# State-space layer with two routed tokens on one core: another order of the same steps on all engines

## The chip, the core and the metric

The kernel runs on one core of a Trainium2 chip. Its engines each take instructions from a queue of their own, in order: TensorE (PE in the profile), VectorE (DVE), ScalarE (ACT), GpSimd (POOL) and SyncE (SP), which here issues nearly all transfers. What counts is the device time of one execution in microseconds, as the median of the runs. The core runs alone, and the granted clock of TensorE stands at full speed throughout the profile.

## What is computed

The input x has 2048 tokens of 1024 features, the output the same. The reference, cut to what matters (bfloat16 inputs, recurrence over time in its exact form):

```python
xn = layernorm(x)
Lam_bar = exp(dt * Lam); B_bar = ((Lam_bar - 1) / Lam)[:, None] * B     # complex, 1024 states
for t in range(2048):
    h = Lam_bar * h + (B_bar @ xn[t])
    a[t] = 2 * real(C @ h) + xn[t] * Dskip
r = xn @ w_r;  idx = the two tokens with the largest r
b = xn;  b[idx] += sigmoid(r[idx]) * ((silu(xn[idx] @ w_gate) * (xn[idx] @ w_up)) @ w_down)
y = x + a + b
```

## The kernel before, in words

**Stages.** The tokens go through in 8 frames of 256 and 16 chunks of 128. Of frame f, `Bu.f.j` (TensorE, L667, 16 matmuls, eight groups j) multiplies the normalised, transposed tokens by B; `u.f.j` (ScalarE, L673) copies the result from PSUM; `TI.f` (VectorE, L722 and L724) turns it by a table of phases, so that the recurrence becomes a real one. Of chunk c, `SC.c.0.0` and `SC.c.0.1` (VectorE, L750; L743 for chunk 15) are the scans of the real and the imaginary part; `gb.c` (ScalarE, L756) copies each to bfloat16; `cw`, `cy` and `cin` (GpSimd, L766, L774, L781 and L782) carry the state to the next chunk, whose scan needs it; `TO.c` (VectorE, L792 and L794, in pieces of half the groups or less for chunks 0, 1 and 15 at L799 to L801) turns the states back; `Y.c.q` (TensorE, L879, 8 matmuls) multiplies them by C, into one of three PSUM banks that `seed.c.h` (ScalarE, L855) has filled with the residual. `xs.c` (ScalarE, L864) and `xm.c` (VectorE, L869) form the skip term in one of two output buffers, `ADD.c.h` (VectorE, L890) adds half a chunk of the product to it, and `out.c.h` (SP, L894) stores the half. The buffers of `xs.c` are those of chunk c-2, so `xs.c` needs the stores of c-2 landed. The seed that takes a bank needs the addition that emptied it.

**Layer norm.** Chunks 0 to 5 have their statistics on VectorE (`bs`, `bn`, L309 and L312) and are normalised there (`apply`, L338 and L345); of the others ScalarE does both (`sum`, `sq`, `apply`, L318, L324 and L349). `rstd` (L277, L278), `nmean`, `nmr` and `nmr1` are small steps on ScalarE or GpSimd. The first four chunks are transposed by TensorE (`Tpe`, L382 and L387) and copied by ScalarE (`xnT`, L394), the later ones by a transposing transfer on SP (`T.c`, L400). B is transposed by transfers as well (`B.j`, L234). The tables of phases and decay come from small vectors (`pcol`, `wr`, `dt`, `frq`, `sin`, `first`, `cos`, `inv`, `rc`, ...); `rc.0` (VectorE, L547) needs `inv.0` (ScalarE, L543 and L544).

**The two tokens.** `r.f` (TensorE, L408) scores all tokens with the column that `wr` (VectorE, L486) made; `cand` and `idx` (VectorE) find the best two; `gather` (GpSimd, L991) fetches their rows, `xz` (GpSimd, L1017) clears a tile; `bns` (VectorE, L283 and L285), `rstds` (ScalarE, L277 and L278) and `norm` (VectorE, L1012) normalise them, `sT` (SP, L1023) transposes them. The expert weights come in 42 loads `w.n` (SP, L1055 and L1059) and are used in eight visits `mm.i` (TensorE, L1071 and L1102), with `exp`, `gu` and `gT` (ScalarE and VectorE) between. `rows` (ScalarE, L1114) scales the result, `row_.q` (SP, L1117) moves its pieces into one tile. For chunk 15 a product with a selecting matrix adds it in PSUM (`hotY`, L884); for all others `fix` (GpSimd, L1121) adds the two rows to the output by an accumulating transfer, which needs every store of chunks 0 to 14 landed and all pieces moved. The stores of chunk 15 follow it.

**What sets the order.** Every step above is a task with a name. A constant `ORDER` (L25 to L65) lists all tasks by hand; `run` asserts that each stands behind what it needs, and `emit` (L98) issues the instructions of each task in that order. Since the schedule is manual (L125), each engine's queue is the list cut to that engine's tasks, and an engine waits at a task whose input is not ready, with all later ones queued behind it. Semaphores follow the data, so a changed order changes no result.

```python
    def emit(self):
        for n in self.order:
            self.tasks[n]["fn"]()
```

Of the kernel before, what the change touches and what calls it, by code (L numbers as in the profile page):

```python
# [17 lines left out]
T = 128  # L18
# [4 lines left out]
EPS = 1e-5  # L23
NREP = 4
ORDER = """  # L25
x.0 x.1 xa pre start.0 warm.0 warm.1 Bn.1 bs.0 bn.0 rstd.0 nmean.0 nmr1.0 bs.1 applyA apply.0 bn.1 warm.2 warm.3 warm.4 warm.5 warm.6 warm.7 warm.8
warm.9 warm.10 warm.11 warm.12 warm.13 warm.14 warm.15 x.2 TpeA x.3 Tpe.0 xnT0 pP.0 pcol.0 wr xnT.0 Bn.0 tB.0 bs.2 tB.1 rstd.1 apply.1 B.0.0 B.0.1
Tpe.1 Bh.0.0.0 Bh.0.0.1 nmean.1 xnT.1 bs.3 bn.2 rstd.2 nmr1.1 bn.3 nmean.3 B.1.0 apply.2 Bh.0.1.0 B.1.1 Bu.0.0 dt frq Tpe.2 rstd.3 apply.3 Bh.0.1.1
Tpe.3 turns x.4 whole angle abs den B.4.0 Bu.0.1 u.0.0 rad xnT.2 B.2.0 Bh.1.0.0 xnT.3 B.2.1 nmean.2 nmr.2 nmr.0 trig sin B.3.0 first u.0.1 Bh.1.0.1
Bu.1.0 Bu.1.1 Bu.1.2 cos bs.4 bn.4 nmr.1 x.5 bs.5 bn.5 nmr1.3 sq1.0 sq1.1 nmr.3 B.3.1 kappa B.4.1 nmean.4 nmean.5 B.5.0 B.5.1 x.6 B.6.0 u.1.0 B.6.1  # L30
B.7.0 Bu.1.3 u.1.1 log inv.0 rc.0 R0.0 tan.0 u.1.2 inv.1 rc.1 tan.1 B.7.1 cs ts.0.1 u.1.3 rstd.5 rstd.4 apply.4 T.4 xr.0 R0.1 R.1 R.0 Bu.0.2 Bu.0.3
Bu.0.4 nmr1.2 u.0.2 u.0.3 ntan.0 ntan.1 TI.0.0 x.7 E2c.1 xr.2 u.0.4 Bu.0.5 Bu.0.6 sum.6 Bu.0.7 nmean.6 nmr.5 nmr1.4 ends cin.0.0 apply.5 x.9 x.8 u.0.5
T.5 u.0.6 Bu.1.4 xnT.4 SC.0.0.0 nmr.4 sq.6 nmr1.5 SC.0.0.1 Bu.1.5 u.0.7 xs.0 TI.0.4 xnT.5 rstd.6 nmr.6 apply.6 T.6 u.1.4 u.1.5 C.0.0 cw.0.0 cy.0.0
xnT.6 Drow seed.0.0 seed.0.1 ts.0.0 E2c.0 ts.1.0 Bu.1.6 Bu.1.7 Bu.2.0 u.1.6 u.1.7 Bu.2.1 gb.0.0.0 x.12 gb.0.0.1 Bu.2.2 E2n.0 u.2.0 u.2.1 Bu.2.3 Bu.2.4
xr.1 sum.7 u.2.2 Bu.2.5 cin.0.4 SC.0.4.0 gb.0.4.0 SC.0.4.1 C.0.1 cin.1.0 SC.1.0.0 gb.0.4.1 ts.1.1 E2s.1 E2s.0 SC.1.0.1 E2n.1 TO.0.0 TO.0.4 cw.0.4
cy.0.4 u.2.3 Bu.2.6 nmean.7 sq.7 u.2.4 Bu.2.7 rstd.7 nmr.7 apply.7 T.7 gb.1.0.0 cin.1.4 cw.1.0 cy.1.0 xs.1 gb.1.0.1 C.1.0 u.2.5 u.2.6 SC.1.4.0 xm.0
SC.1.4.1 TO.1.0 gb.1.4.0 gb.1.4.1 E2t.1 TO.1.4 u.2.7 sum.9 TI.1.0 C.1.1 sum.8 E2t.0 Y.0.0 Y.0.1 cw.1.4 cy.1.4 cin.2.0 xnT.7 Bu.3.0 seed.1.0 nmean.9
sq.9 nmean.8 rstd.9 Bu.3.1 nmr.9 apply.9 Bu.3.2 u.3.0 u.3.1 cin.2.4 SC.2.0.0 gb.2.0.0 SC.2.0.1 ADD.0.0 sq.8 xm.1 Y.0.2 Y.1.0 Y.1.1 x.10 cw.2.0
gb.2.0.1 Y.0.3 seed.1.1 T.9 sum.12 nmean.12 u.3.2 ADD.1.0 ADD.0.1 out.0.0 TO.2.0 Bu.3.3 Bu.3.4 u.3.3 rstd.8 nmr.8 seed.2.0 Y.1.2 out.0.1 xs.2 Bu.3.5
Bu.3.6 apply.8 w.0 w.1 seed.2.1 T.8 x.15 u.3.4 sq.12 rstd.12 x.11 nmr.12 out.1.0 Y.2.0 Y.2.1 xr.3 cy.2.0 cin.3.0 SC.3.0.0 SC.3.0.1 cw.3.0 cy.3.0 u.3.5  # L40
gb.3.0.0 gb.3.0.1 Y.1.3 cin.4.0 u.3.6 nmr1.6 TI.2.0 ADD.1.1 xm.2 ADD.2.0 apply.12 x.14 sum.10 nmean.10 sq.10 xr.4 SC.4.0.0 cw.4.0 T.12 out.2.0 xnT.9
Bu.3.7 SC.4.0.1 TO.3.0 u.3.7 Y.2.2 rstd.10 nmr.10 gb.4.0.0 xnT.8 Y.2.3 gb.4.0.1 ADD.2.1 TO.4.0 Bu.4.0 Bu.4.1 cy.4.0 cin.5.0 SC.5.0.0 cw.5.0 u.4.0
out.1.1 Bu.4.2 apply.10 T.10 seed.3.0 u.4.1 Bu.4.3 u.4.2 Y.3.0 Y.3.1 sum.11 xs.3 Bu.4.4 Bu.4.5 nmean.11 out.2.1 seed.3.1 seed.4.0 xr.5 SC.5.0.1 sum.15
cy.5.0 cin.6.0 sq.11 nmr1.10 xm.3 gb.5.0.0 rstd.11 ADD.3.0 xs.4 TI.3.0 Y.3.2 Y.3.3 xm.4 seed.4.1 u.4.3 u.4.4 gb.5.0.1 ADD.3.1 x.13 nmean.15 SC.6.0.0
nmr.11 SC.6.0.1 sq.15 rstd.15 Y.4.0 nmr.15 apply.11 apply.15 TO.5.0 gb.6.0.0 Y.4.1 Bu.4.6 u.4.5 Y.4.2 seed.5.0 gb.6.0.1 ADD.4.0 u.4.6 cw.6.0 TO.6.0
Y.4.3 cy.6.0 nmr1.12 cin.7.0 xr.6 SC.7.0.0 cw.7.0 Bu.4.7 ADD.4.1 SC.7.0.1 cy.7.0 cin.8.0 T.11 xnT.11 sum.14 nmean.14 sq.14 xnT.10 Bu.5.0 seed.5.1
u.5.0 Y.5.0 Y.5.1 Y.5.2 Y.5.3 out.3.0 u.4.7 out.3.1 xs.5 xm.5 ADD.5.0 ADD.5.1 T.15 rstd.14 nmr.14 apply.14 TI.4.0 seed.6.0 nmr1.15 gb.7.0.0 xr.7 T.14
Bu.5.1 gb.7.0.1 sum.13 nmean.13 sq.13 rstd.13 nmr.13 out.4.0 Y.6.0 apply.13 Y.6.1 SC.8.0.0 xnT.14 seed.6.1 Bu.5.2 Bu.5.3 u.5.1 SC.8.0.1 Y.6.2 Bu.5.4
out.4.1 out.5.1 u.5.2 TO.7.0 nmr1.11 T.13 xnT.13 xnT.12 cw.8.0 out.5.0 xnT.15 nmr1.9 r.0 cy.8.0 u.5.3 u.5.4 cin.9.0 cand gb.8.0.1 idx Bu.5.5 Y.6.3
nmr1.14 xs.6 xr.8 gb.8.0.0 nmr1.8 xm.6 ADD.6.0 nmr1.7 xs.7 SC.9.0.0 Bu.5.6 Bu.5.7 SC.9.0.1 ADD.6.1 gather w.2 nmr1.13 xz w.3 u.5.5 u.5.6 w.4 u.5.7  # L50
TI.5.0 w.5 seed.7.0 seed.7.1 xr.9 w.6 bns Bu.6.0 Bu.6.1 u.6.0 seed.8.0 Bu.6.2 gb.9.0.1 u.6.1 w.7 xm.7 rstds Y.7.0 Y.7.1 cw.9.0 cy.9.0 out.6.1 out.6.0
ADD.7.0 cin.10.0 Y.7.2 Y.7.3 u.6.2 norm sT ADD.7.1 out.7.1 gb.9.0.0 Bu.6.3 out.7.0 xT ymb0 xs.8 TO.8.0 Bu.6.4 seed.8.1 sig SC.10.0.0 xr.10 xm.8 Bu.6.5
seed.9.0 SC.10.0.1 u.6.3 gb.10.0.0 u.6.4 mm.0 Y.8.0 Y.8.1 ADD.8.0 xs.9 TO.9.0 u.6.5 Y.8.2 Bu.6.6 cw.10.0 cy.10.0 cin.11.0 w.8 w.9 w.10 w.11 out.8.0
seed.9.1 gb.10.0.1 Y.8.3 sig1 xm.9 mm.1 ADD.8.1 SC.11.0.0 SC.11.0.1 u.6.6 exp.0 TO.10.0 cw.11.0 gu.0 gT.0 Bu.6.7 Bu.7.0 Bu.7.1 u.7.0 u.6.7 gb.11.0.0
gb.11.0.1 Y.9.0 hot w.12 w.13 Y.9.1 Y.9.2 out.8.1 w.14 ADD.9.0 w.15 w.16 xs.10 u.7.1 seed.10.0 seed.10.1 cy.11.0 w.17 mm.2 w.18 w.19 exp.1 xr.11 w.20
Bu.7.2 Bu.7.3 w.21 TI.6.0 Y.10.0 u.7.2 Y.9.3 Y.10.1 cin.12.0 SC.12.0.0 Y.10.2 SC.12.0.1 ADD.9.1 seed.11.0 Y.10.3 xm.10 ADD.10.0 gu.1 w.22 w.23 w.24
w.25 TO.11.0 gb.12.0.1 gb.12.0.0 cw.12.0 mm.3 seed.11.1 cy.12.0 ADD.10.1 cin.13.0 SC.13.0.0 SC.13.0.1 out.9.1 out.10.0 gT.1 exp.2 gu.2 gT.2 xr.12
Bu.7.4 Bu.7.5 u.7.3 out.9.0 xs.11 w.26 Y.11.0 Y.11.1 w.27 gb.13.0.1 out.10.1 mm.4 u.7.4 w.28 xm.11 ADD.11.0 cw.13.0 cy.13.0 cin.14.0 Bu.7.6 Bu.7.7
u.7.5 TO.12.0 gb.13.0.0 TO.13.0 Y.11.2 Y.11.3 ADD.11.1 seed.12.0 seed.12.1 xr.13 exp.3 xs.12 u.7.6 Y.12.0 u.7.7 Y.12.1 xm.12 w.29 seed.13.0 w.30 w.31
TI.7.0 ADD.12.0 seed.13.1 w.32 SC.14.0.0 SC.14.0.1 cw.14.0 gb.14.0.0 gb.14.0.1 w.33 w.34 w.35 gu.3 mm.5 Y.12.2 Y.12.3 out.11.0 ADD.12.1 Y.13.0 Y.13.1  # L60
TO.14.0 xr.14 out.11.1 xs.13 seed.14.0 w.36 w.37 gT.3 Y.13.2 Y.13.3 xm.13 ADD.13.0 ADD.13.1 w.38 w.39 w.40 w.41 mm.6 Y.14.0 mm.7 Y.14.1 cy.14.0 xr.15
out.12.1 seed.14.1 cin.15.0 out.12.0 SC.15.6.0 rows xs.14 seed.15.0 out.13.0 out.13.1 SC.15.0.0 SC.15.0.1 TO.15.0 xm.14 ADD.14.0 row_.1 Y.14.2 Y.14.3
ADD.14.1 row_.2 SC.15.4.0 row_.3 ymb xs.15 SC.15.4.1 TO.15.4 Y.15.0 out.14.0 out.14.1 SC.15.6.1 TO.15.6 seed.15.1 hotY.15.0 xm.15 seed.15.2 Y.15.1 fix
Y.15.2 Y.15.3 Y.15.4 Y.15.5 Y.15.6 hotY.15.2 Y.15.7 ADD.15.0 hotY.15.1 ADD.15.1 out.15.0 out.15.1 Y.15.8 ADD.15.2 out.15.2
"""  # L65


# [1116 lines left out]
```

## Time and profile before

| | us |
|---|---|
| median of 3 runs | 252.13 |
| lowest and highest run | 251.70, 252.75 |
| the profiled execution | 251.76 |
| its span in the profile | 250.0 |
| TensorE busy | 243.9 |
| VectorE busy | 238.9 |
| ScalarE busy | 175.8 |
| GpSimd busy | 92.5 |

The span runs from the first to the last instruction on the core; 1.76 us of the execution lie around it. Busy time is the union of an engine's instructions, which overlap a little at their ends; a start and a duration in a row are in microseconds from the start of the span. A row of several instructions of a line (x32) gives first start and total length. A wait in brackets is the idle time of the engine ahead of that row, with what ended it.

### The profile page before, as it was taken

What the parts mean: (1) busy time and instruction counts of PE and PEld (TensorE: products, weight loads), DVE (VectorE), ACT (ScalarE), POOL (GpSimd) and SP (SyncE); (2) the same over time, 40 slices, a digit from 0 to 9 for tenths busy, and PEclk for the clock granted to TensorE, in tenths of its full rate; (3) what the DMA queues carried; (4) which work ended last, traced back from release to release, by engine and by line L of the source; (5) the groups of instructions that cost most, each with busy time, mean ns of one, the idle gap of its engine ahead of it and who ended that gap; (6) DMA issues with size and microseconds to landing.
All of it is one profiled execution on the core that took longest, in us unless ns stands there. A gap on an engine that the chain in (4) does not pass through costs nothing.

```text
span 250.0 us, 5063 instructions
## 1 busy us (share of the span) xinstructions
PE 243.9 (98%) x1985; PEld 164.5 (66%) x1985; DVE 238.9 (96%) x281; ACT 175.8 (70%) x303; POOL 92.5 (37%) x133
## 2 busy tenths in 40 slices
PE   7899999999999999999999999999999999999995
PEld 5798888867575686556567784745756467444453
DVE  6997999999999999999999999999999999999995
ACT  2999897989799989989796843656560559215640
POOL 4352534532417490727024539206532331004001
PEclk9999999999999999999999999999999999999999
DMA  6999979989357625132422476088899799779211
GB/s 212 248 202 198 196 214 233 247 173 233 86 161 223 122 72 138 47 84 42 75 74 66 166 250 217 17 283 300 281 330 357 231 321 388 282 244 293 97 45 43
DMA packets 66757, 46.82 MB, mean 187 GB/s; under 512 B 46115, under 2 KB 52649, under 8 KB 66733
## 3 DMA queue, kind: packets, MB, share of 16 engines
q1 hardware_dynamic: 66444, 46.41, 66.3%
q8 instruction: 15, 0.25, 0.4%
q10 hardware_dynamic: 192, 0.07, 0.1%
q14 instruction: 10, 0.07, 0.1%
q0 software_dynamic: 96, 0.01, 0.1%
HBM read 31.21 MB, written 4.20 MB: 142 GB/s over the span
## 4 chain that ended last, share of the span: by engine, by line
PE 72%; DVE 23%; issue 2%; DMA 1%; SPq 0%; DVEq 0%
PE pY L879 34%; PE pB L667 34%; DVE gf L750 7%; DVE m L792 4%; DVE ot L890 2%; PE pG L1071 2%; DVE v L724 2%; DVE m L722 2%; PE pD L1102 1%; DMA xt<-in_A_x_dram 1%; DVE hT L794 1%; DVE ot L869 1%; PE pT L382 1%; DVE st L309 0%; DVE st L283 0%
## 5 line engine op out<-in xcount | busy, mean ns | idle before, releaser
L667 PE MATMUL pB<-xnT,BT 128*128 128x256 bf16 (+1 forms) x1072 | 115.8, 268 | 0.0
L879 PE MATMUL pY<-CT,hT 128*128 128x512 bf16 (+1 forms) x528 | 114.7, 373 | 0.2 <-DVE hT L794 0.2
L667 PEld LDWEIGHTS <-BT 128*128 128x128 bf16 x1072 | 100.4, 98 | 15.9 <-issue 1.7
L879 PEld LDWEIGHTS <-hT 128*128 128x128 bf16 x528 | 51.1, 98 | 56.2 <-DVE hT L794 1.0
L766 POOL TENSOR_TENSOR cw<-gf,tL 128x16 f32<-128x16 f32 (+1 forms) x34 | 44.1, 1297 | 111.9 <-DVE gf L750 111.1
L750 DVE TENSOR_TENSOR_SCAN gf<-R,v 128x1040 f32<-128x1040 f32 (+1 forms) x34 | 68.7, 2056 | 0.4
L855 ACT ACTIVATE pY<-xr,nmr_all,rstd_all 128x512 f32<-128x512 bf16 (+1 forms) x33 | 25.0, 764 | 27.7 <-DVE ot L890 27.7
L756 ACT CAST gb<-gf 128x1024 bf16<-128x1024 f32 (+1 forms) x34 | 31.6, 943 | 15.1 <-DVE gf L750 13.8
L673 ACT CAST u<-pB 128x512 bf16<-128x512 f32 x64 | 35.5, 577 | 8.8 <-PE pB L667 8.5
L792 DVE TENSOR_TENSOR m<-gb,E 128x4096 bf16<-128x4096 bf16 x13 | 29.7, 2286 | 0.1
L890 DVE TENSOR_TENSOR ot<-pY,ot 128x512 bf16<-128x512 f32 (+1 forms) x33 | 21.6, 667 | 1.4 <-PE pY L879 0.5
L864 ACT ACTIVATE ot<-xr,nmr_all,rstd_all 128x1024 bf16<-128x1024 bf16 x16 | 19.8, 1236 | 0.1
L794 DVE TENSOR_TENSOR hT<-m 128x2048 bf16<-128x2048 bf16 x13 | 15.9, 1225 | 0.4
L724 DVE TENSOR_TENSOR v<-u,m 128x4096 bf16<-128x4096 bf16 x7 | 16.0, 2292 | 0.2
L722 DVE TENSOR_TENSOR m<-u,E1t 128x4096 bf16<-128x4096 bf16 x7 | 16.0, 2280 | 0.0
L349 ACT ACTIVATE xn<-xt,nmr_all,rstd_all 128x1024 bf16<-128x1024 bf16 x10 | 12.3, 1236 | 0.2
L324 ACT ACTIVATE xn<-xt,nmean_all 128x1024 bf16<-128x1024 bf16 x10 | 11.5, 1146 | 0.2
L774 POOL TENSOR_TENSOR cy<-cw 128x16 f32<-128x16 f32 (+1 forms) x17 | 11.0, 644 | 1.3
L869 DVE TENSOR_TENSOR ot<-ot,Drow 128x1024 bf16<-128x1024 bf16 x16 | 10.8, 676 | 0.0
L782 POOL TENSOR_TENSOR v<-cy,v 128x16 bf16<-128x16 f32 (+1 forms) x17 | 10.3, 606 | 1.4
L318 ACT ACTIVATE xn<-xt 128x1024 bf16<-128x1024 bf16 x10 | 10.5, 1054 | 0.0
L781 POOL CAST v<-cy 128x16 bf16<-128x16 f32 (+1 forms) x17 | 9.9, 583 | 0.9
(155 smaller groups left out, 169.1 us busy)
## 6 DMA issues: line engine op xcount, KB each, us to landing
wt<-in_B_w_gate_dram SPq DMA_DIRECT2D x14, 512.0 KB, 6.9
wt<-in_B_w_up_dram SPq DMA_DIRECT2D x14, 512.0 KB, 7.6
xr<-in_A_x_dram SPq DMA_DIRECT2D x16, 256.0 KB, 3.6
wt<-in_B_w_down_dram SPq DMA_DIRECT2D x4, 1024.0 KB
out_dram<-ot SPq DMA_DIRECT2D x31, 128.0 KB, 2.0
xt<-in_A_x_dram SPq DMA_DIRECT2D x15, 256.0 KB, 3.1
wt<-in_B_w_down_dram SPq DMA_DIRECT2D x6, 512.0 KB, 6.1
xt<-in_A_x_dram SPq DMA_DIRECT2D x2, 128.0 KB, 2.3
```

Of the source, the lines that this page charges most:

```text
L667: nc.tensor.matmul(out=pB[:, ri, ts_], lhsT=BT[ri][j][:, k, :], rhs=xnT_frame(f)[:, k, ts_], start=(k == 0), stop=(k == DT - 1))
L673: nc.scalar.copy(out=u_tiles[f][:, :, :, j, :].rearrange("p c i t -> p i c t"), in_=pB_tiles.pop((f, j))[:].rearrange("p i (c t) -> p i c ...
L722: nc.vector.tensor_tensor(out=m[:].rearrange("p c i j t -> p c (i j t)"), in0=u[:].rearrange("p c i j t -> p c (i j t)"), in1=E1t[:].rearr ...
L724: nc.vector.tensor_add(out=v[:, :, :, :, 2:], in0=u[:], in1=m[:, :, ::-1])
L750: nc.vector.tensor_tensor_scan(out=flat(gf), data0=flat(R[:, js, :]), data1=flat(v[:, ri, js, :]), initial=0.0, op0=ALU.mult, op1=ALU.add)
L756: nc.scalar.copy(out=gb_tiles[c][:, ri, js, :], in_=gf_tiles[c, js.start, ri][:, :, 2:])
L766: nc.gpsimd.tensor_tensor(out=cw_tiles[c, js.start][:, ri, :, 0:n], in0=g.unsqueeze(1).to_broadcast([128, 2, n]), in1=tL[:, ri, :, js], op ...
L792: nc.vector.tensor_tensor(out=m[:].rearrange("p k i j t -> p k (i j t)"), in1=E2[:].rearrange("p k i j t -> p k (i j t)"), in0=flat(gb[:]) ...
L855: nc.scalar.activation(out=pY[:, 0:d_.stop - d_.start], in_=y_tiles["xr", c][:, d_], func=ACT.Identity, bias=nmr_all[:, c:c + 1], scale=rs ...
L864: nc.scalar.activation(out=y_tiles["ot", c][:], in_=y_tiles["xr", c][:], func=ACT.Identity, bias=nmr_all[:, c:c + 1], scale=rstd_all[:, c: ...
L879: nc.tensor.matmul(out=pY, lhsT=h_tiles[c][:, ri, j, :], rhs=CT[ri][h][:, j, d0:d0 + w], start=False, stop=end, skip_group_check=True)
L890: nc.vector.tensor_add(out=ot, in0=y_tiles.pop(("pY", c, dh))[:, 0:d_.stop - d_.start], in1=ot)
```

## The change

Only the constant `ORDER` is another one; the tasks, their code and their engines are the same, so that each queue holds the same instructions in another sequence. What moves:

- **Start.** `wr` goes from just behind `pcol.0` to behind `bn.5`; `frq` stands ahead of `apply.2`; `Tpe.2` and `Tpe.3` are neighbours; `u.0.1` stands ahead of `sin` and no longer between `first` and `cos`. On SP the transpose `T.5` stands ahead of `B.6` and `B.7` instead of behind them, and `x.7` earlier.
- **Chunks 0 to 5.** On ScalarE `gb.1.0.1` stands 16 places later. On VectorE `TO.1.0` stands behind `SC.2.0.0` and `ADD.0.0` ahead of it; `ADD.4.0` comes ahead of `TO.5.0`; `TI.2.0` stands directly ahead of `SC.4.0.0`; on GpSimd `nmr1.5` and `nmr.2` stand between `cw.3.0` and `cy.3.0`. The pieces of `TO.0` and `TO.1` and the scans around them are reordered.
- **Selected tokens.** `r.0` stands three read-out groups earlier and two `Bu` groups later; `cand` and `idx` stand ahead of `SC.8.0.1`; `gather`, `bns`, `rstds`, `norm` and `sT` are earlier, with `norm` directly behind `bns` on VectorE, ahead of `SC.9.0.0`.
- **Expert visits.** `mm.0` to `mm.3` stand earlier against the other products, `mm.5` and `mm.7` within one group of where they were; `gT.2` is later.
- **Chunks 12 to 15.** On SP `out.10.1` stands directly behind the loads `w.31`, `w.32` and `w.33`; on ScalarE `xs.12` stands between `seed.12.1` and `u.7.7`, with `u.7.6` ahead of it. On VectorE `ADD.14.0` and `ADD.14.1` stand between scans of chunk 15. On SP the last stores and rows go `out.13.0 row_.2 row_.3 out.13.1 out.14.1 row_.1 out.14.0 out.15.0 out.15.2`. The last product on TensorE is `hotY.15.2`.

The diff, cut (the list is read across the lines; both halves are the old and the new constant):

```diff
...
-warm.9 warm.10 warm.11 warm.12 warm.13 warm.14 warm.15 x.2 TpeA x.3 Tpe.0 xnT0 pP.0 pcol.0 wr xnT.0 Bn.0 tB.0 bs.2 tB.1 rstd.1 apply.1 B.0.0 B.0.1
...
-Tpe.3 turns x.4 whole angle abs den B.4.0 Bu.0.1 u.0.0 rad xnT.2 B.2.0 Bh.1.0.0 xnT.3 B.2.1 nmean.2 nmr.2 nmr.0 trig sin B.3.0 first u.0.1 Bh.1.0.1
-Bu.1.0 Bu.1.1 Bu.1.2 cos bs.4 bn.4 nmr.1 x.5 bs.5 bn.5 nmr1.3 sq1.0 sq1.1 nmr.3 B.3.1 kappa B.4.1 nmean.4 nmean.5 B.5.0 B.5.1 x.6 B.6.0 u.1.0 B.6.1
-B.7.0 Bu.1.3 u.1.1 log inv.0 rc.0 R0.0 tan.0 u.1.2 inv.1 rc.1 tan.1 B.7.1 cs ts.0.1 u.1.3 rstd.5 rstd.4 apply.4 T.4 xr.0 R0.1 R.1 R.0 Bu.0.2 Bu.0.3
-Bu.0.4 nmr1.2 u.0.2 u.0.3 ntan.0 ntan.1 TI.0.0 x.7 E2c.1 xr.2 u.0.4 Bu.0.5 Bu.0.6 sum.6 Bu.0.7 nmean.6 nmr.5 nmr1.4 ends cin.0.0 apply.5 x.9 x.8 u.0.5
-T.5 u.0.6 Bu.1.4 xnT.4 SC.0.0.0 nmr.4 sq.6 nmr1.5 SC.0.0.1 Bu.1.5 u.0.7 xs.0 TI.0.4 xnT.5 rstd.6 nmr.6 apply.6 T.6 u.1.4 u.1.5 C.0.0 cw.0.0 cy.0.0
...
-cy.0.4 u.2.3 Bu.2.6 nmean.7 sq.7 u.2.4 Bu.2.7 rstd.7 nmr.7 apply.7 T.7 gb.1.0.0 cin.1.4 cw.1.0 cy.1.0 xs.1 gb.1.0.1 C.1.0 u.2.5 u.2.6 SC.1.4.0 xm.0
-SC.1.4.1 TO.1.0 gb.1.4.0 gb.1.4.1 E2t.1 TO.1.4 u.2.7 sum.9 TI.1.0 C.1.1 sum.8 E2t.0 Y.0.0 Y.0.1 cw.1.4 cy.1.4 cin.2.0 xnT.7 Bu.3.0 seed.1.0 nmean.9
-sq.9 nmean.8 rstd.9 Bu.3.1 nmr.9 apply.9 Bu.3.2 u.3.0 u.3.1 cin.2.4 SC.2.0.0 gb.2.0.0 SC.2.0.1 ADD.0.0 sq.8 xm.1 Y.0.2 Y.1.0 Y.1.1 x.10 cw.2.0
...
-Bu.3.6 apply.8 w.0 w.1 seed.2.1 T.8 x.15 u.3.4 sq.12 rstd.12 x.11 nmr.12 out.1.0 Y.2.0 Y.2.1 xr.3 cy.2.0 cin.3.0 SC.3.0.0 SC.3.0.1 cw.3.0 cy.3.0 u.3.5
-gb.3.0.0 gb.3.0.1 Y.1.3 cin.4.0 u.3.6 nmr1.6 TI.2.0 ADD.1.1 xm.2 ADD.2.0 apply.12 x.14 sum.10 nmean.10 sq.10 xr.4 SC.4.0.0 cw.4.0 T.12 out.2.0 xnT.9
...
-nmr.11 SC.6.0.1 sq.15 rstd.15 Y.4.0 nmr.15 apply.11 apply.15 TO.5.0 gb.6.0.0 Y.4.1 Bu.4.6 u.4.5 Y.4.2 seed.5.0 gb.6.0.1 ADD.4.0 u.4.6 cw.6.0 TO.6.0
...
-out.4.1 out.5.1 u.5.2 TO.7.0 nmr1.11 T.13 xnT.13 xnT.12 cw.8.0 out.5.0 xnT.15 nmr1.9 r.0 cy.8.0 u.5.3 u.5.4 cin.9.0 cand gb.8.0.1 idx Bu.5.5 Y.6.3
-nmr1.14 xs.6 xr.8 gb.8.0.0 nmr1.8 xm.6 ADD.6.0 nmr1.7 xs.7 SC.9.0.0 Bu.5.6 Bu.5.7 SC.9.0.1 ADD.6.1 gather w.2 nmr1.13 xz w.3 u.5.5 u.5.6 w.4 u.5.7
-TI.5.0 w.5 seed.7.0 seed.7.1 xr.9 w.6 bns Bu.6.0 Bu.6.1 u.6.0 seed.8.0 Bu.6.2 gb.9.0.1 u.6.1 w.7 xm.7 rstds Y.7.0 Y.7.1 cw.9.0 cy.9.0 out.6.1 out.6.0
-ADD.7.0 cin.10.0 Y.7.2 Y.7.3 u.6.2 norm sT ADD.7.1 out.7.1 gb.9.0.0 Bu.6.3 out.7.0 xT ymb0 xs.8 TO.8.0 Bu.6.4 seed.8.1 sig SC.10.0.0 xr.10 xm.8 Bu.6.5
-seed.9.0 SC.10.0.1 u.6.3 gb.10.0.0 u.6.4 mm.0 Y.8.0 Y.8.1 ADD.8.0 xs.9 TO.9.0 u.6.5 Y.8.2 Bu.6.6 cw.10.0 cy.10.0 cin.11.0 w.8 w.9 w.10 w.11 out.8.0
...
-Bu.7.4 Bu.7.5 u.7.3 out.9.0 xs.11 w.26 Y.11.0 Y.11.1 w.27 gb.13.0.1 out.10.1 mm.4 u.7.4 w.28 xm.11 ADD.11.0 cw.13.0 cy.13.0 cin.14.0 Bu.7.6 Bu.7.7
-u.7.5 TO.12.0 gb.13.0.0 TO.13.0 Y.11.2 Y.11.3 ADD.11.1 seed.12.0 seed.12.1 xr.13 exp.3 xs.12 u.7.6 Y.12.0 u.7.7 Y.12.1 xm.12 w.29 seed.13.0 w.30 w.31
-TI.7.0 ADD.12.0 seed.13.1 w.32 SC.14.0.0 SC.14.0.1 cw.14.0 gb.14.0.0 gb.14.0.1 w.33 w.34 w.35 gu.3 mm.5 Y.12.2 Y.12.3 out.11.0 ADD.12.1 Y.13.0 Y.13.1
-TO.14.0 xr.14 out.11.1 xs.13 seed.14.0 w.36 w.37 gT.3 Y.13.2 Y.13.3 xm.13 ADD.13.0 ADD.13.1 w.38 w.39 w.40 w.41 mm.6 Y.14.0 mm.7 Y.14.1 cy.14.0 xr.15
-out.12.1 seed.14.1 cin.15.0 out.12.0 SC.15.6.0 rows xs.14 seed.15.0 out.13.0 out.13.1 SC.15.0.0 SC.15.0.1 TO.15.0 xm.14 ADD.14.0 row_.1 Y.14.2 Y.14.3
-ADD.14.1 row_.2 SC.15.4.0 row_.3 ymb xs.15 SC.15.4.1 TO.15.4 Y.15.0 out.14.0 out.14.1 SC.15.6.1 TO.15.6 seed.15.1 hotY.15.0 xm.15 seed.15.2 Y.15.1 fix
-Y.15.2 Y.15.3 Y.15.4 Y.15.5 Y.15.6 hotY.15.2 Y.15.7 ADD.15.0 hotY.15.1 ADD.15.1 out.15.0 out.15.1 Y.15.8 ADD.15.2 out.15.2
...
+Tpe.3 xnT.3 nmean.3 nmr.0 turns whole angle abs x.4 u.0.0 Bh.0.1.1 Bu.0.1 u.0.1 bs.5 den B.3.1 bn.5 B.4.0 B.4.1 Bh.1.0.0 Bh.1.0.1 Bu.1.0 Bu.1.1 Bu.1.2
+wr sin first cos u.1.0 log sq1.0 sq1.1 bs.4 B.5.0 x.7 u.1.1 inv.0 rstd.5 u.1.2 Bu.0.2 kappa inv.1 u.0.2 bn.4 Bu.1.3 u.1.3 Bu.1.4 u.1.4 rc.0 B.5.1
+apply.5 tan.0 T.5 R0.0 xnT.5 rc.1 rstd.4 tan.1 cs R.0 apply.4 Bu.0.3 u.0.3 Bu.0.4 Bu.0.5 B.6.0 ntan.0 u.0.4 sum.7 ts.0.0 R0.1 ts.1.1 TI.0.0 B.6.1
+Bu.1.5 B.7.0 B.7.1 nmean.2 nmr1.2 ends nmean.7 u.0.5 sq.7 u.1.5 x.6 Bu.0.6 Bu.1.6 Bu.0.7 nmean.4 rstd.7 nmr.7 ts.0.1 nmr1.3 E2c.0 R.1 T.4 xnT.4
...
+cw.1.4 seed.0.1 Bu.3.1 Y.0.0 Y.0.1 cy.1.4 sum.9 u.2.7 Bu.3.2 nmean.9 sq.9 rstd.9 xs.0 xm.0 C.1.0 ADD.0.0 rstd.8 u.3.0 seed.1.0 gb.1.0.1 nmr.8 u.3.1
+u.3.2 cy.1.0 cin.2.4 Y.0.2 Bu.3.3 E2t.1 Bu.3.4 xs.1 apply.8 C.1.1 Y.0.3 cin.2.0 SC.2.0.0 SC.2.0.1 cw.2.0 cy.2.0 cin.3.0 T.8 seed.1.1 gb.2.0.0 gb.2.0.1
+out.0.0 x.12 nmr.9 x.10 x.11 xr.2 u.3.3 xm.1 sum.12 apply.9 nmean.12 TO.1.0 TO.2.0 Bu.3.5 SC.3.0.0 SC.3.0.1 Y.1.0 Y.1.1 nmr.3 cw.3.0 Bu.3.6 ADD.0.1
+ADD.1.0 xnT.8 T.9 x.13 nmr1.5 out.1.0 xnT.9 nmr.2 sq.12 rstd.12 u.3.4 nmr.12 Y.1.2 u.3.5 u.3.6 gb.3.0.0 gb.3.0.1 Bu.3.7 cy.3.0 seed.2.0 Y.1.3 u.3.7
+apply.12 seed.2.1 xr.3 T.12 out.0.1 sum.10 sum.11 Bu.4.0 Bu.4.1 Y.2.0 Y.2.1 Bu.4.2 xs.2 nmean.10 cin.4.0 TI.2.0 SC.4.0.0 SC.4.0.1 cw.4.0 nmr.4 ADD.1.1
...
+xm.4 ADD.4.0 TO.5.0 Y.4.2 Y.4.3 apply.13 T.13 xs.5 gb.6.0.1 u.4.6 gb.6.0.0 seed.5.0 cy.6.0 cin.7.0 SC.7.0.0 SC.7.0.1 cw.7.0 u.4.7 sq.15 u.5.0 Y.5.0
...
+Bu.5.6 T.14 u.5.4 u.5.5 seed.6.1 u.5.6 xs.6 ADD.5.1 xnT.14 TO.7.0 r.0 Bu.5.7 Bu.6.0 Y.6.0 cand idx xm.6 w.2 w.3 w.4 w.5 u.5.7 xr.8 cw.8.0 seed.7.0
+gb.8.0.0 SC.8.0.1 gather Y.6.1 ADD.6.0 gb.8.0.1 u.6.0 xz cy.8.0 cin.9.0 out.5.0 bns rstds norm SC.9.0.0 sT sig nmr1.14 Bu.6.1 u.6.1 gb.9.0.0 nmr1.12
+Y.6.2 Y.6.3 Bu.6.2 ADD.6.1 Y.7.0 Bu.6.3 cw.9.0 out.6.1 w.6 out.5.1 u.6.2 Bu.6.4 xT mm.0 sig1 SC.9.0.1 xs.7 Y.7.1 cy.9.0 ymb0 cin.10.0 u.6.3 TO.8.0
...
+Y.10.3 ADD.10.1 gb.13.0.0 u.7.3 u.7.4 gu.2 Y.11.0 Y.11.1 seed.11.1 xr.12 gb.13.0.1 u.7.5 w.28 w.29 out.10.0 mm.4 w.30 Y.11.2 xr.13 w.31 w.32 w.33
+out.10.1 ADD.11.0 TO.12.0 out.11.0 w.34 w.35 Bu.7.6 u.7.6 Bu.7.7 cw.13.0 seed.12.0 cy.13.0 cin.14.0 seed.12.1 Y.11.3 TO.13.0 Y.12.0 ADD.11.1 gT.2 mm.5
+xs.12 u.7.7 seed.13.0 Y.12.1 Y.12.2 Y.12.3 exp.3 nmr1.15 TI.7.0 SC.14.0.0 xm.12 ADD.12.0 SC.14.0.1 xr.14 gu.3 ADD.12.1 gb.14.0.0 w.36 out.11.1 w.37
+w.38 out.12.0 w.39 w.40 w.41 seed.13.1 gb.14.0.1 xs.13 seed.14.0 out.12.1 xr.15 xs.14 Y.13.0 Y.13.1 Y.13.2 TO.14.0 xm.13 gT.3 cw.14.0 cy.14.0 cin.15.0
+Y.13.3 ADD.13.0 SC.15.0.0 xm.14 mm.6 ADD.13.1 SC.15.4.0 seed.14.1 seed.15.0 Y.14.0 Y.14.1 SC.15.0.1 TO.15.0 mm.7 Y.14.2 Y.14.3 rows out.13.0 row_.2
+row_.3 out.13.1 ADD.14.0 SC.15.4.1 ADD.14.1 out.14.1 seed.15.1 SC.15.6.0 row_.1 ymb TO.15.4 SC.15.6.1 seed.15.2 Y.15.0 Y.15.1 Y.15.2 Y.15.3 Y.15.4
+TO.15.6 Y.15.5 Y.15.6 hotY.15.0 xs.15 xm.15 ADD.15.0 hotY.15.1 out.14.0 fix Y.15.7 Y.15.8 out.15.0 ADD.15.1 out.15.1 hotY.15.2 ADD.15.2 out.15.2
```

## Rows read from the trace of the kernel before

**Rows 1.** The page, part 1: busy time, share of the span, instructions
```profile
PE 243.9 (98%) x1985; PEld 164.5 (66%) x1985; DVE 238.9 (96%) x281; ACT 175.8 (70%) x303; POOL 92.5 (37%) x133
```

**Rows 2.** The list of waits: total, times, longest (us)
```profile
DVE gf L547 <- ACT gf L544: 1.1, 1, 1.1
```

**Rows 3.** Timeline of PE, 95 to 170: start, duration, work, [wait before it]
```profile
116.58 7.08 PE L879 MATMUL pY<-CT,hT 128*128 128x512 bf16 x32
...
162.40 1.48 PE L1071 MATMUL pG<-wt,mw 128*32 128x512 bf16 x24 [0.23 <-DMA mw<-xnsel]
164.12 5.35 PE L879 MATMUL pY<-CT,hT 128*128 128x512 bf16 x24 [0.25 <-DVE hT L794]
```

**Rows 4.** The chain that ended last: start, its time, engine, tile, line
```profile
115.30 1.22 DVE hT L794
```

**Rows 5.** Timelines of DVE, PE and POOL, 222 to 250
```profile
230.14 1.22 DVE L794 TENSOR_TENSOR hT<-m 128x2048 bf16<-128x2048 bf16 x1
...
231.71 1.90 PE L879 MATMUL pY<-CT,hT 128*128 128x512 bf16 x8
...
243.51 1.40 POOL L1121 DMA_INDIRECT out_dram<-ymb,idx_t  x1 [15.54 <-issue]
```

**Rows 6.** Timeline of all engines, 0 to 16
```profile
9.26 1.01 ACT L394 COPY xnT<-pT 128x1024 bf16<-128x1024 bf16 x1
```

**Rows 7.** DMA issues: KB each where known, median us to landing
```profile
BT<-in_A_B_re_dram SPq DMA_TRANSPOSE x7, 4.7
...
xsel<-in_A_x_dram,idx_t POOLq DMA_INDIRECT x1, 2.4
```

**Rows 8.** Timeline of PE, 22 to 40
```profile
21.78 18.41 PE L667 MATMUL pB<-xnT,BT 128*128 128x256 bf16 x166
```

**Rows 9.** Timelines of ACT and DVE, 54 to 66
```profile
61.10 0.19 ACT L324 ACTIVATION_READ_ACCUMULATOR xn<-xt,nmean_all 128x1 f32 x1
...
63.58 4.54 DVE L750 TENSOR_TENSOR_SCAN gf<-R,v 128x1040 f32<-128x1040 f32 x2
```

**Rows 10.** Timeline of all engines, 67.9 to 70.2
```profile
68.03 0.67 DVE L890 TENSOR_TENSOR ot<-pY,ot 128x512 bf16<-128x512 f32 x1
...
68.49 0.22 POOL L774 TENSOR_TENSOR cy<-cw 128x16 f32<-128x16 f32 x1
68.61 0.68 DVE L869 TENSOR_TENSOR ot<-ot,Drow 128x1024 bf16<-128x1024 bf16 x1
...
68.78 0.64 POOL L781 CAST v<-cy 128x16 bf16<-128x16 f32 x1
...
69.40 1.29 DVE L890 TENSOR_TENSOR ot<-pY,ot 128x512 bf16<-128x512 f32 x2
```

**Rows 11.** Timelines of DVE, POOL and all engines, around the selected tokens
```profile
145.81 0.69 DVE L869 TENSOR_TENSOR ot<-ot,Drow 128x1024 bf16<-128x1024 bf16 x1
...
146.87 1.02 POOL L991 DMA_INDIRECT xsel<-in_A_x_dram,idx_t  x1 [5.83 <-PE pB L667]
...
158.00 0.20 DVE L285 BATCH_NORM_AGGREGATE mv<-st 2x2 f32<-2x12 f32 x1
...
158.56 0.20 ACT L278 ACTIVATE rstd_s<-lv 2x1 f32<-2x1 f32 x1
```

**Rows 12.** Timeline of SP, 235 to 250 (shorter windows keep the stores apart)
```profile
235.30 2.48 SPq L1117 DMA_DIRECT2D ymb<-ym  x3
...
240.50 0.33 SPq L894 DMA_DIRECT2D out_dram<-ot  x1
...
246.64 1.16 SPq L894 DMA_DIRECT2D out_dram<-ot  x2
```

**Rows 13.** The instructions of line L894: from issue to landing
```profile
DMA to landing us min/median/max: 1.6/1.9/8.8
```

**Rows 14.** Timelines of SP and ACT, 205 to 222
```profile
209.08 0.45 SPq L894 DMA_DIRECT2D out_dram<-ot  x1
...
211.26 1.24 ACT L864 ACTIVATE ot<-xr,nmr_all,rstd_all 128x1024 bf16<-128x1024 bf16 x1
```

## What the change does to the time, predicted

> **What bounds it now.** The page's first part comes first: TensorE is busy for 243.9 us of a span of 250.0, VectorE for 238.9 [rows 1]. Both are full, so the question is not which engine is shortened but which waits and holes stand in two nearly closed rows of work. The list of waits names what is left: VectorE's longest wait in the middle is one of 1.1 us, for a scalar result of the tables [rows 2]. TensorE's timeline then shows two waits, 0.23 us where the expert visits begin (for the selected tokens' transposed rows) and 0.25 us where chunk 8's read-out begins (for its turned states) [rows 3]. The chain of waits shows where VectorE hands over: the turn of chunk 5 ends 0.06 us before TensorE reads it [rows 4], and near the end the turn of chunk 14 ends at 231.36 with TensorE taking it at 231.71 [rows 5]. At these two places the engines run level, and a VectorE that comes later there holds TensorE up one for one. The end hangs on a third thing: the accumulating transfer of the selected rows ("fix") needs all stores of chunks 0 to 14 landed, and the last chunk's stores stand behind it.
>
> The profiled execution took 251.76 us, its span 250.0, and 1.76 lie around it. It is 0.37 under the median of 252.13; I sum against the execution and add 0.37 at the end. A measurement of this kernel tells about 0.5% from no change: 1.26 us.
>
> **What stays.** No instruction is added or removed. Listing each engine's tasks by name, ahead of chunk 5's read-out and again ahead of chunk 14's, TensorE has the same set of work in both orders; VectorE has the same set ahead of the turn of chunk 14, and one addition more (ADD.4.0, 0.6 of pitch) ahead of the turn of chunk 5. So the sum consists of waits and holes alone.
>
> **The start.** The cast of w_r leaves VectorE's way to apply.1, which could give 0.26, but Bu.0.0 needs the copy xnT.1 on ScalarE, which ends at 10.27 [rows 6] behind the same ScalarE work. I take -0.05; bounds 0 and -0.26.
>
> **Tables.** Between "first" and "cos" ScalarE no longer runs u.0.1, so the reciprocal that VectorE waits 1.1 for comes one cast, 0.54, earlier: -0.54 on VectorE, bounds 0 and -1.1.
>
> **SP's queue at the start.** The transpose T.5 now stands ahead of B.6's and B.7's and waits for apply.5, which I place near 22.4, so these come some 4 us later; they land 4.7 after issue [rows 7]. TensorE reaches Bu.0.6 and Bu.0.7, its users, near 31.1 and 34.6, by counting groups of 16 matmuls at 1.75 through the row of 166 without a wait [rows 8]; I place the landings near 30 and 32.5. Cost 0 while this cover of 0.5 to 2 us stands; without it up to +1.
>
> **Holes on VectorE.** A multiplication xm and the addition ADD that needs it leave a hole of 0.11 as neighbours (68.61+0.68 to 69.40 [rows 10]), where independent neighbours overlap by about 0.08. The new order parts three of eight such pairs ahead of the turn of chunk 14, and some pairs of scan and turn. I take -0.5 by the turn of chunk 5 and -0.95 by that of chunk 14; bounds 0 and these.
>
> **New waits on VectorE.** (a) SC.2.0.0 now needs gb.1.0.1, which stands 16 ScalarE tasks later. ScalarE would reach its end near 62.4: the work up to 61.28, less about 1.65 (xs.1, a table copy), plus about 2.8 (sq.8, small ones, a cast). VectorE, which began SC.2.0.0 at 63.58 [rows 9], now has the three turn steps of TO.1.0 (-1.9) behind it, ADD.0.0 (+0.6) before it and the gains above, and comes near 61.1. The bounds are 0 and +1.3; since ScalarE's own waits of that stretch shrink, I take +0.3. (b) The gather moves with idx: the scan SC.8.0.1 (2.27, half of the row of two [rows 9]) no longer stands ahead of it and VectorE leads by about 0.7, so 146.87 becomes 143.9 [rows 11], and it lands 2.4 later [rows 7], at 146.3. VectorE comes to bns, behind xm.6, SC.8.0.1 and ADD.6.0, at 146.3 too: I take +0.1, bounds 0 and +1.0. On POOL only xz and cy.8.0 stand behind the gather. (c) norm now follows bns directly and waits for the two ScalarE steps of rstds: from 158.20 to 158.76 [rows 11], and 0.1 for the lost overlap, +0.7 (bounds 0 and +0.7). Behind norm wait SC.9.0.0 and, through sT, the first visit. (d) SC.4.0.0 follows TI.2.0 directly and needs GpSimd's cin.4.0, which now has nmr1.5, nmr.2 and cy.3.0 ahead of it. In the trace a GpSimd step with two inputs in SBUF began at 68.49 under an addition that reads PSUM, and the multiplication of two SBUF operands began at 68.61 beside it, held by nothing; the next GpSimd step, L781, took 0.64 and ended with that multiplication [rows 10]. As ADDs surround cy.3.0 and cin.4.0, I take 0; bounds 0 and +0.6.
>
> The Trainium skill, "SBUF — State Buffer", section "Who interferes with whom", says that a VectorE step with two SBUF inputs and a GpSimd step that reads SBUF share a port pair: "Whoever issues first gets the shared pair for the whole instruction". The row at 68.61, which began 0.10 before the GpSimd step ended, does not show VectorE blocked. By that rule (d) would add an estimated 0.25 to 0.5, and chunk 5's turn would come that much later.
>
> **The middle.** norm comes some 12 us earlier and the first visit 7.5 us earlier, so its input lies ready about 4 us ahead; chunk 8's turn moves 3 to 5 us ahead of its read-out. With neighbours overlapping by 0.07, TensorE gains 0.30+0.32 = -0.62. The same slack covers (b) and (c) at this point, but they stay in VectorE's own sum.
>
> **Sum at the two level places.** Turn of chunk 5: 116.52+0.6-0.54-0.5+0.3 = 116.4, against 116.5 for TensorE: a margin of 0.1. Turn of chunk 14: 231.36-0.54-0.95+0.3+0.1+0.7 = 231.0, against 231.71-0.62 = 231.1: a margin of 0.1. So TensorE keeps its -0.62 on both, narrowly.
>
> **The tail.** Of chunk 14 the second half is now stored first, and the last store, out.14.0, is issued behind out.14.1 (0.33) and row_.1 (0.83, a third of 2.48 [rows 12]). VectorE's work from the turn of chunk 14 to ADD.14.1 was 9.1 (to 240.47, just ahead of the store at 240.50 [rows 12]); SC.15.4.0 and SC.15.4.1 come in and SC.15.6.0 goes out, +0.6, holes -0.3: 9.4. So ADD.14.1 ends at 240.4 and out.14.0 is issued at 241.6. From the last such store to the landed fix it took 5.86 in the trace (240.50, fix at 243.51 [rows 5], landed at 246.36, when out.15.0 could be released [rows 12]). That makes 247.46, then 0.33 and a gap for out.15.0, and out.15.2 is issued at 247.87 against 247.47 (246.64+1.16-0.33): **+0.4**, though VectorE's last addition is over some 0.5 earlier. Profile 251.76+0.4 = 252.16; on the scale of the median **252.5**. Its own bounds are 251.6, if the store of out.14.0 is not held, and 253.3, with waits of 0.8 more passed on.
>
> **Rivals.** (B) The tail holds nothing: row_.1 and out.14.1 pass quickly or the fix lands sooner, and TensorE's -0.62 plus the end of VectorE decides: -0.56, 251.6. For it speaks that the 3 us from store to fix issue were one sample. (C) Slower: xs.12 on ScalarE must wait until out.10.1 has landed, since the output buffers are two. That store now stands on SP directly behind the expert-weight loads w.31 to w.33; I place its issue near 208.4. It comes ahead of u.7.7, which TI.7.0 needs; before, xs.12 had begun at 211.26 [rows 14], without a wait. VectorE will be at TI.7.0 near 215.6, by the sum of its work. Stores land 1.9 after issue in the median, the slowest 8.8 [rows 13]; the row at 209.08, which stands behind such loads [rows 14], is that one. xs.12 (1.24) and a cast follow the landing, so it decides from a landing at 213.7; at 215.5 it costs 1.8-0.2 = +1.6, giving 254.0; at the full 8.8, +3.2, 255.6. The Trainium skill, "DMA: Bandwidth & Descriptors", section "Queues, rings and completion order", states that descriptors of one ring are consumed in order, which would put the store behind the loads' bytes; the row at 209.08 agrees with it. Against it: at the loads' rate I estimate the landing at 212.5. (D) Small waits at (a), (b) and (d) come out at their upper ends and, with a margin of 0.1 at chunks 5 and 14, pass to TensorE: about +0.8 over the forecast, 253.3. (F) The start's 0.26, the middle's 0.62 and the tail's idle time all come back: 250.7. That the change doesn't do what it says is no rival: the order is issued as written.
>
> **How the numbers follow.** Forecast 0.38, B 0.20, C 0.14, D 0.20 (half of it within 0.5%), F 0.08. Faster by over 0.5%: F, 0.08. Within: 0.38+0.20+0.10 = 0.68. Slower: C and half of D, 0.24. The range reaches from between B and F, 251.1, to C's nearer end, 254.2; it leaves out half of F and more than half of C.
>
> **What would show it.** Right: no wait at the first visit nor at chunk 8; TensorE's chunk 14 near 231.1; the fix landing near 247.5 and out.15.2 issued behind it; VectorE's wait at the reciprocal near 0.6; a wait of 0.6 at norm. Wrong: TensorE waits for turned states at chunk 5 or 14, or for u.7.7's scans; Bu.0.6 waits for its table; or a VectorE wait of over 1 us at SC.2.0.0 or bns.

## The result, and the profile after

The changed kernel takes **254.8 us** in the median of 6 runs (254.42 to 255.83), the kernel before 252.16 in as many runs beside it: a ratio of 1.0108, with a 95% interval of 1.0081 to 1.0135. It is slower by 2.6 us in the medians, and lies above the forecast of 252.5 and its range, which ended at 254.2. The profiled execution took 254.74, its span 253.0 against 250.0 before.

The first part of the page and the chain of waits by engine stand against [rows 1]:

```profile
PE 244.5 (97%) x1985; PEld 165.0 (65%) x1985; DVE 238.6 (94%) x281; ACT 174.2 (69%) x303; POOL 87.2 (34%) x133
...
DVE 59%; ACT 15%; issue 9%; PE 7%; DMA 5%; POOL 3%; SPq 0%; DVEq 0%; POOLq 0%
```

TensorE's busy time is 0.6 us longer and VectorE's 0.3 shorter than before; neither explains 3 us of span. The difference is idle time: what the two engines did not lose before, they lose now. The chain that ended last ran over TensorE for 72% of the span before; now VectorE carries 59% of it and TensorE 7%. VectorE became the bound. The list of waits (total, times, longest) says where, to be read beside [rows 2]:

```profile
DVE st L283 <- DMA xsel<-in_A_x_dram,idx_t: 1.4, 1, 1.4
...
PE pY L879 <- DVE hT L794: 1.2, 2, 1.1
...
PE pY L879 <- ACT pY L855: 0.8, 2, 0.5
...
DVE gf L547 <- ACT gf L544: 0.8, 1, 0.8
...
DVE xnsel L1012 <- ACT sig L996: 0.7, 1, 0.7
```

VectorE waits 1.4 us at `bns` for the gathered rows, where it had not waited at all, and 0.7 at `norm`. The wait at `rc.0` fell to 0.8. TensorE's timeline shows what came of it; these rows answer to [rows 3, 5]:

```profile
117.20 1.90 PE L879 MATMUL pY<-CT,hT 128*128 128x512 bf16 x8 [0.15 <-DVE hT L794]
...
155.77 1.48 PE L1071 MATMUL pG<-wt,mw 128*32 128x512 bf16 x24
...
163.04 3.61 PE L879 MATMUL pY<-CT,hT 128*128 128x512 bf16 x16 [0.46 <-ACT pY L855]
...
197.39 1.89 PE L879 MATMUL pY<-CT,hT 128*128 128x512 bf16 x8 [0.30 <-ACT pY L855]
...
233.86 3.63 PE L879 MATMUL pY<-CT,hT 128*128 128x512 bf16 x16 [1.06 <-DVE hT L794]
```

The first visit (155.77) and chunk 8 no longer wait for the tokens or the turned states: the 0.62 that the forecast counted is there. But chunk 5 waits 0.15 for its turn, chunks 8 and 10 wait 0.46 and 0.30 for a seed that ScalarE wrote late, and chunk 14 waits 1.06 for its turn. That turn ended at 231.36 before [rows 5] and ends at 233.8 now, where the forecast had 231.0. Its last step in the chain that ended last, as in [rows 4]:

```profile
232.58 1.24 DVE hT L794
```

**Where VectorE lost it.** Worked out task by task (its start, less the time that all that stands ahead of it on its queue took in the kernel before), VectorE is about 0.5 us behind the old order at apply.3, has made this up by the tables, and leads by 0.1 to 0.3 at SC.8.0.1 (by durations, or by distances between starts). It is 2.0 behind at ADD.6.1, one `bns` and one `norm` later, and 2.4 at the turn of chunk 14. The timeline around the gather shows the 2.1 us at a glance:

```profile
143.26 0.14 DVE L978 CAST idx_t<-tok 32x1 uint32<-32x1 f32 x1
143.37 0.69 DVE L869 TENSOR_TENSOR ot<-ot,Drow 128x1024 bf16<-128x1024 bf16 x1
143.97 2.32 DVE L750 TENSOR_TENSOR_SCAN gf<-R,v 128x1040 f32<-128x1040 f32 x1
144.43 2.70 POOL L991 DMA_INDIRECT xsel<-in_A_x_dram,idx_t  x1 [12.41 <-DMA out_dram<-ot]
146.32 0.69 DVE L890 TENSOR_TENSOR ot<-pY,ot 128x512 bf16<-128x512 f32 x1
...
148.45 1.28 DVE L283 BATCH_NORM_STATS2 st<-xsel 2x6 f32<-2x512 bf16 x2 [1.44 <-DMA xsel<-in_A_x_dram,idx_t]
149.76 0.20 DVE L285 BATCH_NORM_AGGREGATE mv<-st 2x2 f32<-2x12 f32 x1
...
150.61 0.54 DVE L1012 TENSOR_SCALAR xnsel<-xsel,mv,rstd_s 2x1024 bf16<-2x1024 bf16 x1 [0.65 <-ACT sig L996]
```

The gather starts 1.03 us behind idx (143.40 to 144.43), as before. It starts 0.46 into the scan SC.8.0.1, and its row is 2.70 us long, where it was 1.02 [rows 11]: it ends 0.84 behind the scan's end at 146.29. The rows land 1.30 later, VectorE waits 1.44 for them, then 0.65 more for `rstds`. (The last row names `sig`, the next ScalarE step, which `norm` does not read; rstds' second step ended at 150.52.)

**The tail.** SP's last stores and the accumulating transfer, against [rows 5, 12]:

```profile
243.14 0.33 SPq L894 DMA_DIRECT2D out_dram<-ot  x1
243.53 0.60 SPq L1117 DMA_DIRECT2D ymb<-ym  x1
...
244.17 0.40 SPq L894 DMA_DIRECT2D out_dram<-ot  x1
...
249.91 0.81 SPq L894 DMA_DIRECT2D out_dram<-ot  x2
...
247.19 1.41 POOL L1121 DMA_INDIRECT out_dram<-ymb,idx_t  x1 [16.77 <-issue]
```

The last store of chunk 14 goes out 1.03 behind the one before it, fix starts 3.0 later as it did before, out.15.0 is released at 249.91, and the last store follows near 250.3, though its addition had ended at 249.55. The tail costs 0.8 us beyond VectorE's end; before it cost nothing.

### The profile page after: what moved, and what is told of

Read it like the earlier page. It is cut to its first block, busy times and chain, and to the rows that moved or that the text cites. A ratio compares the mean times of both kernels' runs of the same rounds, so it can differ in the third digit from the quotient of the medians.

```text
span 253.0 us, 5068 instructions
## 1 busy us (share of the span) xinstructions
PE 244.5 (97%) x1985; PEld 165.0 (65%) x1985; DVE 238.6 (94%) x281; ACT 174.2 (69%) x303; POOL 87.2 (34%) x133
## 3 DMA queue, kind: packets, MB, share of 16 engines
q1 hardware_dynamic: 66444, 46.41, 67.9%
## 4 chain that ended last, share of the span: by engine, by line
DVE 59%; ACT 15%; issue 9%; PE 7%; DMA 5%; POOL 3%; SPq 0%; DVEq 0%; POOLq 0%
DVE gf L750 19%; DVE m L792 11%; PE pY L879 6%; DVE ot L890 5%; DVE v L724 4%; DVE m L722 4%; DVE hT L794 4%; ACT u L673 3%; DVE ot L869 3%; ACT gb L756 2%; DMA out_dram<-ot 2%; DMA xsel<-in_A_x_dram,idx_t 2%; ACT xn L324 1%; DMA xt<-in_A_x_dram 1%; DVE ts L598 1%
## 5 line engine op out<-in xcount | busy, mean ns | idle before, releaser
L879 PE MATMUL pY<-CT,hT 128*128 128x512 bf16 (+1 forms) x528 | 116.2, 373 | 2.0 <-DVE hT L794 1.2
L766 POOL TENSOR_TENSOR cw<-gf,tL 128x16 f32<-128x16 f32 (+1 forms) x34 | 30.7, 903 | 108.0 <-DVE gf L750 107.4
L673 ACT CAST u<-pB 128x512 bf16<-128x512 f32 x64 | 36.2, 578 | 10.7 <-PE pB L667 10.5
L782 POOL TENSOR_TENSOR v<-cy,v 128x16 bf16<-128x16 f32 (+1 forms) x17 | 21.0, 1233 | 1.4
L309 DVE BATCH_NORM_STATS2 st<-xt 128x6 f32<-128x512 bf16 x12 | 7.9, 680 | 1.1 <-DMA xt<-in_A_x_dram 1.1
```

The source lines that it names most:

```text
L673: nc.scalar.copy(out=u_tiles[f][:, :, :, j, :].rearrange("p c i t -> p i c t"), in_=pB_tiles.pop((f, j))[:].rearrange("p i (c t) -> p i c ...
L766: nc.gpsimd.tensor_tensor(out=cw_tiles[c, js.start][:, ri, :, 0:n], in0=g.unsqueeze(1).to_broadcast([128, 2, n]), in1=tL[:, ri, :, js], op ...
L879: nc.tensor.matmul(out=pY, lhsT=h_tiles[c][:, ri, j, :], rhs=CT[ri][h][:, j, d0:d0 + w], start=False, stop=end, skip_group_check=True)
```

## The experiments

Nine kernels ran. Where a diff is shown, it is the list of tasks, cut to the tokens that move.

**1. The addition ahead of the scan.** Theory S: a VectorE step with two operands in SBUF holds the gather's instruction on GpSimd. Theory D: the gather is late because of the transfers beside it.

```diff
...
-seed.7.0 gb.8.0.0 SC.8.0.1 gather Y.6.1 ADD.6.0 gb.8.0.1
+seed.7.0 gb.8.0.0 gather Y.6.1 ADD.6.0 SC.8.0.1 gb.8.0.1
...
```

> The changed kernel with one swap on VectorE: ADD.6.0 ahead of the scan SC.8.0.1, so that the gather on GpSimd begins beside an addition that reads PSUM and not in the middle of a scan. Theory S (the scan, with two operands in SBUF, holds the gather's instruction on GpSimd): the gather's row falls from 2.70 us to about 1.0, its landing from 4.0 to about 2.4 us after its start, VectorE's wait at bns from 1.44 to under 0.3, the turn of chunk 14 ends about 1.4 us earlier, and the time is near 253.3 (1.1 to 1.7 less than the changed kernel's 254.8). Theory D (the gather is late because of the transfers beside it, the weight loads and stores on the rings): the row stays near 2.7, bns still waits 0.7 or more, and the time stays at 254.3 to 254.8.

The timeline of VectorE and GpSimd in it:

```profile
143.77 0.69 DVE L890 TENSOR_TENSOR ot<-pY,ot 128x512 bf16<-128x512 f32 x1
144.38 2.31 DVE L750 TENSOR_TENSOR_SCAN gf<-R,v 128x1040 f32<-128x1040 f32 x1
146.61 1.25 DVE L283 BATCH_NORM_STATS2 st<-xsel 2x6 f32<-2x512 bf16 x2
...
144.03 1.02 POOL L991 DMA_INDIRECT xsel<-in_A_x_dram,idx_t  x1 [12.41 <-DMA xr<-in_A_x_dram]
```

The gather begins beside the addition, and its row is 1.02 again, though the scan starts 0.35 later and covers two thirds of it. bns follows the scan without a wait. Median 253.51, ratio 1.0045 (1.0025 to 1.0064): 1.3 of the 2.6 us are gone, by the swap of two neighbours on one queue, with the same transfers. Theory S holds, D falls. TensorE still waits 0.93 at chunk 14.

**2. The reverse, in the kernel before.** The same swap the wrong way round:

```diff
...
-xm.6 ADD.6.0 nmr1.7 xs.7 SC.9.0.0 Bu.5.6
+xm.6 nmr1.7 xs.7 SC.9.0.0 ADD.6.0 Bu.5.6
...
```

> The kernel before with the reverse swap: the scan SC.9.0.0 ahead of ADD.6.0 on VectorE, so that the gather begins inside a scan. Theory S: the gather's row grows from 1.02 us to 2 to 2.8 and ends after the scan, its landing from 2.4 to about 4 us; nothing waits for it, so the time stays at 252.2. Theory D: the row stays near 1.0.

```profile
146.51 2.32 DVE L750 TENSOR_TENSOR_SCAN gf<-R,v 128x1040 f32<-128x1040 f32 x1
...
146.97 2.69 POOL L991 DMA_INDIRECT xsel<-in_A_x_dram,idx_t  x1 [5.83 <-ACT pY L855]
```

The gather grew from 1.02 to 2.69 us and ends 0.83 behind the scan; it landed 5.4 after its start, later than the expected 4; why its rows came 2.7 behind its end, and not 1.3 as in the changed kernel, is not known. Its one run took 251.85, beside a median of 252.15 for the kernel before: nobody waits for this gather, and holding it shows no cost that one run could tell.

**3. Another step in the scan's place.** In the kernel before, the turn TO.7.0 moved behind idx, so that the gather begins in its first step, a bf16 multiplication:

```diff
...
-out.5.1 u.5.2 TO.7.0 nmr1.11
+out.5.1 u.5.2 nmr1.11
...
-cand gb.8.0.1 idx Bu.5.5
+cand gb.8.0.1 idx TO.7.0 Bu.5.5
...
```

> The kernel before with the turn TO.7.0 (two bf16 steps of 2.3 and 1.2 us, each with two operands in SBUF) behind idx on VectorE, so that the gather, about 1.0 us behind idx, begins inside the first of them. If any such step holds the gather: its row is 1.8 to 3.0 us long and ends 0.8 us behind the end of the step that it began in, or behind the second one. If only the scan does: the row stays at 1.0. The time is no part of this test (VectorE has to wait for the scores of r.0, about 0.9).

```profile
144.59 2.27 DVE L792 TENSOR_TENSOR m<-gb,E 128x4096 bf16<-128x4096 bf16 x1
146.90 1.23 DVE L794 TENSOR_TENSOR hT<-m 128x2048 bf16<-128x2048 bf16 x1
...
145.69 2.07 POOL L991 DMA_INDIRECT xsel<-in_A_x_dram,idx_t  x1 [6.29 <-DMA wt<-in_B_w_up_dram]
```

The row is 2.07 long and ends 0.90 behind the multiplication (146.86), in the middle of the next step, which has two operands in SBUF as well. So it is not a matter of the scan: such a step holds the gather if the gather begins inside it, up to that step's end; a step that begins while the gather already runs does not hold it (runs 1 and 3 show this both). What of the gather is held, its reading of the two indices or its writing of descriptors, these runs don't tell apart. The one run took 253.97, beside 252.07 for the kernel before: VectorE waits 0.90 for the scores of r.0, as expected, and TensorE 1.2 at the first visit; the time was no part of this test.

**4. norm behind a scan.** On top of run 1, norm's wait filled with SC.9.0.0:

```diff
...
-bns rstds norm SC.9.0.0 sT
+bns rstds SC.9.0.0 norm sT
...
```

> The kernel with ADD.6.0 ahead of the scan, and one move more: norm behind the scan SC.9.0.0. If norm's 0.68 us wait for rstds is a part of the loss by itself, VectorE's turn of chunk 14 ends about 0.65 earlier, TensorE's wait for it there falls from 0.93 to about 0.3, and the time is 252.8 to 253.1 (from 253.5). If the later norm makes the first visit wait, TensorE stands at it (a wait of 0.3 or more on the transposed rows) and the time stays near 253.5.

```profile
148.88 0.20 DVE L285 BATCH_NORM_AGGREGATE mv<-st 2x2 f32<-2x12 f32 x1
149.01 2.31 DVE L750 TENSOR_TENSOR_SCAN gf<-R,v 128x1040 f32<-128x1040 f32 x1
151.23 0.51 DVE L1012 TENSOR_SCALAR xnsel<-xsel,mv,rstd_s 2x1024 bf16<-2x1024 bf16 x1
```

No wait at norm, none at the first visit, and TensorE's wait at chunk 14 is gone. Median 252.38, ratio 1.0017 (0.9989 to 1.0045). Run 1 was measured on another chip; each against the kernel before beside it, norm's place is worth 0.7 (by the ratios) to 1.0 us (by the medians), where 0.4 to 0.7 were expected, and the two intervals overlap. The profiles show it more sharply. This execution took 253.19, above its median, and VectorE was already 0.97 behind run 1 at the tables; at ADD.6.1 it was 0.2 behind, and at the turn of chunk 14 it was 0.1 ahead. So about 0.8 is norm, and 0.3 came later; 0.15 of that is a wait at TI.7.0 that run 1 had and this one had not.

**5. The tail alone.** In the changed kernel, row_.1 and out.14.0 moved up:

```diff
...
-row_.2 row_.3 out.13.1 ADD.14.0 SC.15.4.1 ADD.14.1 out.14.1 seed.15.1 SC.15.6.0 row_.1 ymb
+row_.2 row_.3 out.13.1 row_.1 ADD.14.0 out.14.0 SC.15.4.1 ADD.14.1 out.14.1 seed.15.1 SC.15.6.0 ymb
...
-hotY.15.1 out.14.0 fix Y.15.7
+hotY.15.1 fix Y.15.7
...
```

> The changed kernel with two moves at the end of SP's queue: row_.1 ahead of chunk 14's stores, and out.14.0 ahead of out.14.1, as in the kernel before. If the last store of chunk 14 sets when fix lands (the forecast's tail step), that store is issued about 1.0 us earlier (near 243.1), fix starts and lands 1.0 earlier (landing near 248.9), out.15.2 is issued right after its addition near 249.6 and not 250.3, and the time falls by 0.6 to 0.9 us, to about 254.0. Rival: fix is limited by something else (the moved rows, GpSimd's own queue), and the time stays at 254.8.

```profile
246.26 1.40 POOL L1121 DMA_INDIRECT out_dram<-ymb,idx_t  x1 [15.88 <-issue]
...
249.60 0.33 SPq L894 DMA_DIRECT2D out_dram<-ot  x1
```

fix starts 0.93 earlier and the last store 0.74 earlier, right behind its addition. Median 253.88, ratio 1.0056 (1.003 to 1.0082), 0.9 less than the changed kernel, as expected (0.6 to 0.9).

**6. All of it.** Runs 1, 4 and 5 together, and the store out.5.1 ahead of sT on SP (run 7):

> The two edits above together, and two more: norm behind SC.9.0.0 on VectorE, so that its wait for rstds is filled by a scan, and the store out.5.1 ahead of the transfer sT on SP, so that xs.7 on ScalarE doesn't wait for it. If the late gather, norm's wait and the tail are the whole of the loss: VectorE's turn of chunk 14 ends near 231.7, TensorE has no wait there and none at chunk 8's seed, and the time is 252.0 to 252.6, level with the kernel before. If other waits take their place (the first visit waiting for the later norm, TensorE at chunk 14 again), 253 to 254.

TensorE takes chunk 14 without a wait and the end is level with that of before:

```profile
230.24 1.22 DVE L794 TENSOR_TENSOR hT<-m 128x2048 bf16<-128x2048 bf16 x1
...
231.58 3.63 PE L879 MATMUL pY<-CT,hT 128*128 128x512 bf16 x15
...
246.92 0.81 SPq L894 DMA_DIRECT2D out_dram<-ot  x2
```

Median 251.85, a little under the expected 252.0 to 252.6; ratio 0.9988 (0.9963 to 1.0013). The whole loss is undone by four moves within a changed order, and the rest of the change is worth 0.3 us or nothing: no version here is clearly faster than the kernel before.

**7. The store out.5.1 alone**, in the changed kernel, ahead of sT, whose wait for norm holds SP's queue:

```diff
...
-cy.8.0 cin.9.0 out.5.0 bns
+cy.8.0 cin.9.0 out.5.0 out.5.1 bns
...
-out.6.1 w.6 out.5.1 u.6.2
+out.6.1 w.6 u.6.2
...
```

> The changed kernel with the store out.5.1 ahead of the transfer sT on SP, and nothing else. xs.7 on ScalarE no longer waits (3.63 us before), TensorE's wait of 0.46 at chunk 8 for its seed goes. As VectorE, late by bns and norm, decides at chunk 14, TensorE's wait there grows from 1.06 to about 1.5 and the time stays at 254.5 to 254.9. If seeds decide by themselves, the time falls to about 254.3.

```profile
196.93 1.89 PE L879 MATMUL pY<-CT,hT 128*128 128x512 bf16 x8 [0.77 <-ACT pY L855]
...
233.40 3.63 PE L879 MATMUL pY<-CT,hT 128*128 128x512 bf16 x16 [1.06 <-DVE hT L794]
```

The wait at chunk 8 is gone (no row of it is left), the one at chunk 10 grew from 0.30 to 0.77, and chunk 14 waits 1.06 as before. That it would grow to 1.5 was expected and did not come. The one run took 254.35, the time expected if seeds decide by themselves, but that is the start's doing: VectorE was 0.44 ahead of the changed kernel's profile at rc.0 already, and still 0.46 ahead at ADD.14.1. In between the move gained nothing: what TensorE no longer waited at chunk 8 it waited at chunk 10.

**8. The store out.10.1 ahead of the loads w.31 to w.33**, on top of run 6, for the forecast's rival C:

```diff
...
-w.31 w.32 w.33 out.10.1 ADD.11.0
+out.10.1 w.31 w.32 w.33 ADD.11.0
...
```

> The kernel with all four moves, and the store out.10.1 ahead of the weight loads w.31 to w.33 on SP. By the forecast's rival on this store (the store's bytes stand behind the loads): xs.12's wait for it on ScalarE, 1.68 us in the changed kernel, is gone and xs.12 begins right behind seed.12.1; the time doesn't change, since VectorE's TI.7.0 didn't wait. Otherwise xs.12 still waits over 1 us.

xs.12 in the changed kernel, in run 6, and in this one:

```profile
216.21 1.24 ACT L864 ACTIVATE ot<-xr,nmr_all,rstd_all 128x1024 bf16<-128x1024 bf16 x1 [1.68 <-DMA out_dram<-ot]
```

```profile
213.76 1.24 ACT L864 ACTIVATE ot<-xr,nmr_all,rstd_all 128x1024 bf16<-128x1024 bf16 x1 [0.32 <-DMA out_dram<-ot]
```

```profile
213.54 1.23 ACT L864 ACTIVATE ot<-xr,nmr_all,rstd_all 128x1024 bf16<-128x1024 bf16 x1
```

The wait is gone, but the kernel that this run is to be held against is run 6, and there it was 0.32 and not 1.68, so that little was left to take away. Where the store stood, the transfers show: in run 6 it was issued at 208.44 and landed 5.3 later; here it was issued at 206.97, and the last of its 128 packets of 1 KB had moved by 209.18. So it did stand behind the loads. The one run took 251.95, and TI.7.0 waited in neither run, nor in the changed kernel: there it cost nothing.

**9. The start.** On top of run 6, the first tasks in the order before:

> The kernel with all four moves, and its first tasks (up to Tpe.2) in the order of the kernel before. In all four profiles with the new start VectorE waited 0.26 to 0.83 us at bs.1 for the load of token chunk 1, in both profiles with the old start not at all, though the instructions of the first 5 us are the same. If the order of the start makes this, the wait is gone here, TensorE's first group comes near 9.06 and not 9.4, and the time is 251.3 to 251.6. If it is a matter of the run, the wait is still there in some size, and the time stays at 251.85.

bs.1 did not wait in this run, but neither did it in the profiles of runs 4, 7 and 8, which have the new start; there bs.2 waited up to 0.87 instead. Median 252.13, ratio 0.9991 (0.9972 to 1.0009), the same as run 6. Run 3 has the old start, and there bs.1 waited 0.58. When the first token rows land differs by some tenths from run to run; the order does not set it.

## Why the prediction was wrong

**The step that failed** is (b) of the new waits on VectorE: "it lands 2.4 later, at 146.3 ... I take +0.1, bounds 0 and +1.0". The start was right to half a microsecond (143.9 against 144.43), and so was the place; VectorE came to bns 0.7 later than expected (147.0 against 146.3), which made the wait shorter. But the gather was priced with the row of a place where it ran free, and the change moved it into another place: its row grew by 1.68. It landed at 148.43, and the wait was 1.44. The price was in the trace of before, on the same engine, one question away: what does a GpSimd step take when it begins inside a scan?

Two views of the kernel before answer it, the instructions of the carry's line L766 (durations in ns, shortest, median, longest) and the timeline at 65.98:

```profile
L766 POOL TENSOR_TENSOR cw<-gf,tL x34: 220/1110/2194, 34.9 to 226.8; 128x16 f32<-128x16 f32 x26, 128x8 f32<-128x8 f32 x8
```

```profile
65.98 2.15 POOL L766 TENSOR_TENSOR cw<-gf,tL 128x16 f32<-128x16 f32 x1 [7.79 <-DVE gf L750]
```

The same small step takes 0.22 us or 2.19. The one at 65.98 began inside the second of two scans that end at 68.12 [rows 9], and ended with it. It is no exception: of the 26 rows of this line that took over 0.3 us, 25 ended within 0.1 us of the end of the VectorE step in which they began, and the five that began beside an addition that reads PSUM took 0.22. A line on GpSimd whose longest row is ten times its shortest is held in this way here. Read this way, the gather at 143.9 begins inside SC.8.0.1, which the forecast's own sum ends at 145.7 (bns at 146.3 less ADD.6.0); it would end 0 to 1.02 behind that and land 1.4 later (2.4 less 1.02), at 147.1 to 148.1: a wait of 0.8 to 1.8 at bns where +0.1 was taken.

The Trainium skill, "SBUF — State Buffer", section "Who interferes with whom", was weighed at (d), where it mattered little, and not at (b). Its rule that of the two the one that issued first holds the pair for the whole instruction agrees with runs 2 and 3 in one direction: GpSimd waited for VectorE's step. The other direction these runs do not show: in run 1 the scan that began with the gather under way took 2.31 us, as always. The page infers that a two-operand step does not hold up descriptor generation; runs 2 and 3 show a gather held by one. Since a gather also reads its indices from SBUF, they do not tell whether that inference fails or the reading is what is held.

**(c), norm**, was sized right (0.7, measured 0.65) and stood in VectorE's sum.

**The second term that failed is the holes**, taken at -0.95 by the turn of chunk 14, with bounds of 0 and that. Of the 2.8 by which that turn came later than forecast, 1.3 is (b) and 1.2 is this term. VectorE's gaps of under 0.2 us ahead of the turn add up to 4.2 us before and to 4.5 now: the new order parts some pairs and makes others neighbours (18 gaps of 0.07 to 0.18 us, where there were 16). No run tests this term alone, but run 6 bears it out: with the gather free and norm filled its turn ends at 231.46, where the forecast's sum without (b) and (c) gives 230.2; 0.5 of the difference is a load at its start. In the changed kernel, the rest of the 2.8 is 0.4 from a load at the start and 0.2 from the reciprocal, less the 0.3 that (a) did not cost.

**The level places** decided as said. A VectorE that comes later there holds TensorE up one for one: of the 2.4 us, 1.06 became a wait at chunk 14, since TensorE itself had come 1.1 later.

**The tail** was right in mechanism and size: 5.86 from the last store of chunk 14 to the landed fix was forecast, 5.74 measured (244.17 to 249.91), and the last store, forecast 1.0 behind VectorE's end (247.87 against some 246.9), was 0.8 behind it. Rival B, that the tail holds nothing, is out; run 5 shows the price.

**The smaller terms.** The middle's -0.62 came, and was spent on the seeds. rc.0 gave 0.36 (1.12 to 0.76) of the 0.54. Ahead of the gather VectorE led by 0.1 to 0.3, where 0.7 was taken. (a) cost nothing: SC.2.0.0 began at 61.99 without a wait, its copy had ended at 61.82. Nor did (d): cin.4.0 was stretched to 2.28 under the turn TI.2.0, but ended at 80.7, and the hole of 0.13 ahead of SC.4.0.0 at 83.02 stands between TI.4.0 and SC.8.0.0 as well. T.5's cover held, no Bu waited. The start came 0.35 later on TensorE, by a load that VectorE waited 0.42 for.

**Rival C** had the right place and no price: xs.12 waited 1.68 us, VectorE came to TI.7.0 2.9 us later than it was placed, and where it came 1.8 and 2.3 earlier it lost 0.15 there (run 1) or nothing (run 6). **Rival D** is what happened in kind, a VectorE wait above its upper end that passed to TensorE, at three times the size.

## What to carry to other kernels

When a step moves on one engine's queue, look up what runs on the neighbouring engines at its new time, and take its duration from a row with the same neighbour, not from its own old row. On GpSimd above all: a line whose median is five times its shortest row, as that of the carry here, is a sign that VectorE's steps hold it, and a gather on that engine should begin beside a step that reads PSUM, with the long two-operand steps behind it. Nor should a gain be summed from many holes of 0.1 us: the holes that a new order makes have to be counted too. In a kernel with two full engines, look at the queue of the third one for who releases the next input; a swap of two neighbours was worth 1.3 us here, and a whole new order, mended in four places, 0.3 or nothing.

## What was not expected

- A gather that begins inside a VectorE step with two SBUF operands ends 0.83 to 0.90 us behind that step (in three orders, rows of 2.07 to 2.70), and one that begins 0.35 ahead of it takes 1.02.
- The scan does not pay for it: 2.31 to 2.32 us with a gather held or under way, and 2.30 to 2.34 for the others.
- A seed's wait of 0.46 us went in run 7, the next one grew by 0.47, and the wait at chunk 14 stayed at 1.06.
